# Layer 2's input sums formed a superblock ahead and kept in DRAM, and shorter durations assumed by the planner that orders the instructions

## The chip, the cores and the metric

One core of one Trainium2 chip runs the whole program. The metric is device time in microseconds (us) for one launch: 1597.66 us before, the median of 3 runs (1596.65 to 1598.69). TensorE is called PE, VectorE DVE, ScalarE ACT, GpSimd POOL and SyncE SP, as in the profile. SP does nothing but issue DMAs, in one queue, in order.

## The reference

Linear attention, then two multi-layer perceptrons, all in float32:

```python
q_s = softmax(q, axis=-1); k_s = softmax(k, axis=2)     # per head, with 1e-9 in the denominators
kv = einsum('bhsd,bhse->bhde', k_s, v)
x = einsum('bhsd,bhde->bhse', q_s, kv)                  # then heads merged: 4608 tokens x 512
h = x @ w_in1;  x = maximum(0.01 * h, h) @ w_out1       # 512 -> 2048 -> 512
h = x @ w_in2;  out = (h * sigmoid(h)) @ w_out2         # 512 -> 2048 -> 512
```

## The kernel before

The four matrix products are called layers 0 to 3. Every float32 operand is split into a rounded high part and a low part (`split2`: ACT writes the high part, line 302, DVE subtracts it to give the low part, line 298), and each product takes three matmuls (high x high, high x low, low x high). Layer 0 is done plainly (lines 665 to 667, together with the attention). Layers 1, 2 and 3 use a Strassen-like scheme with seven products, numbered 1 to 7, in place of eight. Each product needs its own operand on either side, and three or four of the seven are sums or differences of stored blocks, made by DVE (`add`, line 863).

The 4608 tokens are taken in blocks of 512, and two blocks make a superblock n. There are five, n = 0 to 4, the last with one block. In layer 2 a superblock is 4 turns i over the hidden features, and each turn has the seven products in the order 1, 2, 6, 5, 7, 4, 3. Product 1 of the next turn is pulled ahead of 4 and 3. For n = 0 to 3 each product is 12 matmuls of 512 columns: two output halves rq, two halves kq of the inner dimension, three matmuls each. For n = 4 it is 12 matmuls of 256 columns. So a superblock is 336 matmuls, and layer 2 is 1344 matmuls of 512 columns and 336 of 256 (line 1034).

The x operands of layer 2, one tile for each of 7 products and 2 halves kq, so 14 tiles, stay in SBUF for the whole superblock. The pool `r_x` has 15 such tiles (named x, xr, g, xs, xv in the profile). A tile of the next superblock can be loaded only when the last turn (i = 3) has used the tile whose place it takes.

Before the change `x_all` loads four raw blocks (1, 5, 2, 3) for each kq from the DRAM tensor `x2d`, where layer 1 has stored its output (`store1`, line 997). It loads blocks 1 and 2 a second time, as 11 and 12, into other halves of the tiles. Then DVE forms the other operands, by the table `SUMS["x"]`:

```python
"x": ((7, 3, 5, "-"), (5, 5, 11, "-"), (6, 3, 5, "-"), (4, 12, 6, "-")),
...
yield from operand(keys, "x", r, (1, 5, 3, 2, 6, 7, 4), srcs, lend, home=HOME2, used=ORDER, each=0.5)
```

So 7 = 3 - 5, then the new 5 = 5 - 11, then 6 = 3 - 5 with the new 5, then 4 = 12 - 6. The tiles are taken in the order 1, 5, 3, 2, 6, 7, 4. `split2` of an operand waits for the sums that read it, so 6 waits for the sum that makes 4.

The outputs of layer 2 go bank by bank: ACT copies a PSUM bank or DVE adds it, ACT takes Silu (`active`), and SP stores the result to `gd` (`keep`, line 1098). A bank that carries several products must be read before the next product accumulates into it (`INTO`, `AFTER`).

The order of the instructions on every engine is decided before the launch by a planner (`Queues.run`). Each task is a generator that asks for operations. The planner takes the operation that could start first on its engine, with a rank to break ties, and keeps a clock for each engine that advances by assumed durations: `v_tt`, `v_ts` (DVE), `a_` (ACT), `pe` (PE), 0.73 us to issue a DMA and 3.0 us for it to land. On the chip every queue then runs in that fixed order, and waits on semaphores.

Of the kernel before, what the change touches and what calls it, by code (L numbers as in the profile page):

```python
# [24 lines left out]


def v_tt(n):
    return 0.16 + n / 960


def v_ts(n):
    return 0.16 + n / 1920


def a_(n):
    return 0.19 + n / 1200


def g_tt(n):
# [1 line left out]


def pe(n):
    return 0.007 + n / 2330


def rank(r):
# [7 lines left out]
def wait(*keys):  # L55
    return "wait", keys
# [146 lines left out]
def linear_attention_two_mlps(  # L203
# [28 lines left out]
    P = 128  # L232
# [31 lines left out]
    merge = [2 // len(s) for s in supers]  # L264
    gd1 = [tc.dram_tile([NG, 2, 4, P, len(s), HB], F32, name=f"gda{n}") for n, s in enumerate(supers)]
    gd = [tc.dram_tile([NG, 4, len(s), P, 2, HB], F32, name=f"gd{n}") for n, s in enumerate(supers)]
    x2d = [tc.dram_tile([KD, P, 2, w], F32, name=f"x2d{n}") for n, w in enumerate(width)]

    NKV = 8
    NV = 2 * (D + 1)  # L270
# [422 lines left out]
    def act(j, f, h):  # L693
# [28 lines left out]
    }  # L722
    ORDER = (1, 2, 6, 7, 5, 3, 4)
# [3 lines left out]
    SECOND = (2, 5, 3)  # L727
    HOME = {3: (6, 1), 5: (7, 1), 2: (4, 1)}
    HOMES = HOME, {}
    HOME2 = {11: (5, 0), 12: (4, 1)}  # L730
    slot = {}

    def raw_of(key, c, home):
# [42 lines left out]
    def operand(keys, kind, r, order, srcs, give, home={}, used=(), each=0.0):  # L776

        def turn(c):
            return r + each * used.index(c) if c in used else r

        for key in keys:
            spawn(r, sums(key, kind, home, turn))
        for c in order:
            for key, src in zip(keys, srcs):
                yield rank(r)
                slot[key, c] = yield from give(c)
                done(("slot", key, c))
                for d in src:
                    if home.get(d, (d, 1))[0] == c:
                        spawn(r, fetch(key, d, home, src[d]))  # L790
                spawn(turn(c), split2(key, kind, c, home))
# [6 lines left out]
    def weight(l, i, c):  # L798
# [14 lines left out]
        src = wc[l][2 * i:2 * i + 2, :, PLANS[l][2].index(c)].rearrange("r p n -> p r n")  # L813
        yield from operand([key], "", weight_rank(l, i, c), (c,), [{c: src}], give)

    def x_all():
        for n in range(NJ):

            r, pm = at2[n, 0] - (5 if n else 4), merge[n]
            yield rank(r)  # L820
            yield wait(*(("x2", n, k, t) for k in range(0, KD, pm) for t in range(2)))
            keys, srcs = [], []
            for kq in range(2 // pm):
                keys.append(("x", 2, n, kq))
                srcs.append({})
                for c, k, t in ((1, 0, 0), (5, 0, 1), (2, 1, 0), (3, 1, 1)):
                    at = 2 * k + kq * pm
                    srcs[-1][c] = x2d[n][at:at + pm, :, t].rearrange("k p w -> p k w")
                    if c < 3:
                        srcs[-1][10 + c] = srcs[-1][c]  # L830
            yield from operand(keys, "x", r, (1, 5, 3, 2, 6, 7, 4), srcs, lend, home=HOME2, used=ORDER, each=0.5)

    def g1_all():
        for n in range(NJ):
# [110 lines left out]
                                    spawn(-100, blocks1(n, mb))  # L945

    def blocks1(n, m):
        key, pm = (1, n), merge[n]

        def product(c):  # L950
            yield wait(("p", 1, n, m, c))
            return banks[key, m, c]

        def room():
            return (yield get(r_o))

        def end(c):
            r_b.put(banks.pop((key, m, c)))

        p = yield from product(1)  # L960
        s = yield from room()
        yield op(("A", a_(TB)))
        copy("A", s, p)
        done(("kept", n, m))
        p = yield from product(6)
        yield from add(s, s, p)
        end(6)
        p = yield from product(7)
        u = yield from room()
        yield from add(u, s, p)  # L970
        end(7)
        p = yield from product(4)
        t = yield from room()
        yield from add(t, u, p)
        end(4)
        spawn(-100, store1(n, 2 + m * pm, 0, t))
        p = yield from product(2)
        t = yield from room()
        yield op(("A", a_(TB)))
        copy("A", t, p)  # L980
        banks.pop((key, m, 1))
        end(2)
        spawn(-100, store1(n, m * pm, 0, t))
        p = yield from product(5)
        yield from add(u, u, p)
        spawn(-100, store1(n, 2 + m * pm, 1, u))
        yield from add(s, s, p)
        end(5)
        p = yield from product(3)
        yield from add(s, s, p)  # L990
        end(3)
        spawn(-100, store1(n, m * pm, 1, s))

    def store1(n, k, t, o):
        pm = merge[n]
        yield op(("D", 0.73))
        nc.sync.dma_start(
            out=x2d[n][k:k + pm, :, t].rearrange("k p w -> p k w"), in_=o.rearrange("p (k w) -> p k w", k=pm)
        )
        yield wait()  # L1000
        r_o.put(o)
        done(("x2", n, k, t))

    INTO = {1: 1, 6: 1, 7: 1, 4: 1, 2: 2, 5: 5, 3: 5}
    AFTER = {6: 1, 7: 6, 4: 7, 3: 5}
# [170 lines left out]
    for j in range(NB):  # L1176
        for i in range(NG):
            at3[j, i] = t_
            t_ += 2

    def weight_rank(l, i, c):
        if l == 1:
            return at1[0, int(c in SECOND), i, 0] - 8
        return (at2[0, i] if l == 2 else at3[0, i]) - 8

    with tc.manual_schedule():
        nc.vector.memset(ones, 1.0)
        make_identity(nc, ident)
        nc.scalar.activation(out=small[0]["k"][:, 0:1], in_=ones, func=ACTF.Exp)
        for t_, t in sets:  # L1190
            t5 = t.rearrange("p (c h d) -> p c h d", c=5, h=2)
            nc.gpsimd.memset(t5[:, :, :, D:], 1.0)

            nc.gpsimd.memset(t_[SR:P, 512:640], 0.0)
            nc.gpsimd.memset(t5[SR:P, 4, :, 0:D], 0.0)
        nc.gpsimd.memset(kv_tile, 0.0)

        for n in range(NP):
            r = -40 + 5 * n
            spawn(r, k_task(n))  # L1200
            spawn(r + 1, q_task(n))
            spawn(r + 2, v_task(n))
        for n in range(NP, len(units)):
            b, j, p = units[n]
            r = -12 + 3 * p if j == 1 else step(j, 0) - 14 + 4 * p
            if b is not None:
                spawn(r, k_task(n))
                spawn(r, v_task(n))
            spawn(r, q_task(n))
        for f in range(NF):  # L1210
            spawn(-36 + 6 * f if f < 4 else step(0, f) - 4, split1(f))
            if f < NH:
                spawn(f, layer0(0, f))
        spawn(0, layer0_all())
        for t in (convert1, convert2, convert3):
            spawn(1000, t())
        spawn(0, later())
        for i, c in lead:
            spawn(weight_rank(1, i, c), weight(1, i, c))
        for l in (2, 3):  # L1220
            for i in range(NG):
                for c in ORDER:
                    spawn(weight_rank(l, i, c), weight(l, i, c))
        spawn(base[1] - 4, g1_all())
        spawn(base[2] - 5, x_all())
        spawn(base[3] - 4, g3_all())
        spawn(base[1], layers())
        qs.run()
# [30 lines left out]
```

## Time and profile before

| | |
|---|---|
| median of 3 runs | 1597.66 us |
| the profiled execution's own time | 1598.44 us |
| its span in the profile | 1596.7 us |
| PE busy | 1548.6 us (97%), 9088 matmuls |
| DVE busy | 1093.9 us (69%) |
| ACT busy | 893.5 us (56%) |
| DMA | 320.01 MB, mean 200 GB/s |

Busy time is the time in which an engine has an instruction running. Layer 0 and the attention fill the span up to 507 us, layer 1 (line 931) runs to 855 us, layer 2 (line 1034) to 1230 us, and layer 3 (line 1124) to the end. Clocks are given as a share of full speed: 1.00 is 2.4 GHz, and the lower level is 1.2 GHz.

### The profile page before, as it was taken

The page shows a single profiled execution, that of the slowest core. Times are in us where ns is not written, and L with a number is a line of the kernel's source. Part 1 is how long each engine was busy: PE and PEld are TensorE (multiplying, and loading weights), DVE is VectorE, ACT ScalarE, POOL GpSimd, SP SyncE. Part 2 cuts the span into 40 slices and gives each one's busy share as a digit, 9 for nine tenths or more (in the row PEclk, how much of TensorE's full clock was granted, in tenths as well). Part 3 has the DMA queues.
Part 4 walks back from the last instruction along what each step waited for, and adds up shares of the span by engine and source line. Part 5 has one row for each costly group of instructions (what it writes and reads, how often), then busy time and mean ns, then how long its engine had stood idle before and what let it go on. Part 6 is the DMA issues. An engine that isn't in the chain of part 4 may idle for free.

```text
span 1596.7 us, 26548 instructions
## 1 busy us (share of the span) xinstructions
PE 1548.6 (97%) x9088; PEld 1340.4 (84%) x9088; DVE 1093.9 (69%) x2046; ACT 893.5 (56%) x1965; POOL 39.4 (2%) x56
## 2 busy tenths in 40 slices
PE   5899999999999999999997999999999999999999
PEld 3687888888788888888887878787889999999998
DVE  8986756665656988888888352525267777777774
ACT  7778776685445544454556454545467444444442
POOL 2111000000000000000000000000000000000000
PEclk9999999999999999999999999999999999999999
DMA  8876778786789787878797353535369444444442
GB/s 236 267 200 179 227 228 255 227 269 194 240 268 312 234 293 217 273 219 268 230 323 269 106 185 106 185 106 175 108 195 303 133 131 133 132 133 127 134 128 70
DMA packets 281190, 320.01 MB, mean 200 GB/s; under 512 B 61408, under 2 KB 208352, under 8 KB 281056
## 3 DMA queue, kind: packets, MB, share of 16 engines
q1 hardware_dynamic: 281056, 318.32, 63.8%
q8 instruction: 72, 1.18, 0.3%
q14 instruction: 62, 0.51, 0.1%
HBM read 201.85 MB, written 116.39 MB: 199 GB/s over the span
## 4 chain that ended last, share of the span: by engine, by line
PE 90%; DVE 6%; DMA 2%; SPq 1%; issue 1%; ACT 0%; POOL 0%; DVEq 0%; POOLq 0%; ACTq 0%
PE b L1124 12%; PE h L1124 11%; PE h L1034 10%; PE b L931 10%; PE h L931 10%; PE b L1034 8%; PE h L665 8%; PE h L667 8%; PE h L666 8%; DVE o L863 2%; PE a L637 2%; DVE x L298 1%; PE a L520 1%; PE a L622 1%; DMA u<-in_k_dram 0%
## 5 line engine op out<-in xcount | busy, mean ns | idle before, releaser
L665 PE MATMUL h<-x,w 128*128 128x512 f32 x576 | 237.1, 412 | 1.9 <-ACT w L302 1.1
L666 PE MATMUL h<-x,w 128*128 128x512 f32 x576 | 224.8, 390 | 2.2 <-DVE x L298 1.6
L667 PE MATMUL h<-x,w 128*128 128x512 f32 x576 | 225.2, 391 | 0.4 <-DVE w L298 0.4
L302 ACT ACTIVATE x<-x 128x512 fp32r<-128x512 f32 x194 | 121.6, 630 | 156.8 <-DMA x<-gd 87.7
L863 DVE TENSOR_TENSOR o<-o,h 128x512 f32<-128x512 f32 x107 | 72.3, 686 | 129.1 <-ACT o L302 68.0
L698 ACT ACTIVATE o<-h 128x512 f32<-128x512 f32 x144 | 86.1, 598 | 116.4 <-PE h L667 107.4
L298 DVE TENSOR_TENSOR x<-x 128x512 fp32r<-128x512 f32 x194 | 129.6, 686 | 13.0 <-ACT x L302 10.2
L863 DVE TENSOR_TENSOR o<-o,b 128x512 f32<-128x512 f32 x118 | 79.6, 686 | 85.8 <-ACT o L302 35.4
L665 PEld LDWEIGHTS h<-x,w 128*128 128x128 f32 x576 | 108.4, 188 | 28.0 <-ACT x L645 1.8
L666 PEld LDWEIGHTS h<-x,w 128*128 128x128 f32 x576 | 108.5, 188 | 24.7 <-DVE x L298 3.2
L667 PEld LDWEIGHTS h<-x,w 128*128 128x128 f32 x576 | 108.1, 188 | 24.2 <-DVE w L298 0.8
L1034 PE MATMUL h<-x,a 128*128 128x512 f32 (+1 forms) x489 | 120.8, 379 | 6.9 <-DVE x L298 6.9
L931 PE MATMUL b<-x,a 128*128 128x512 f32 (+1 forms) x498 | 117.6, 374 | 1.2 <-DVE x L298 1.2
L931 PE MATMUL h<-x,a 128*128 128x512 f32 (+1 forms) x510 | 115.0, 364 | 0.5 <-DVE x L298 0.5
L1034 PEld LDWEIGHTS h<-x,a 128*128 128x128 f32 x489 | 88.7, 193 | 24.6 <-DVE x L298 7.7
L1124 PE MATMUL b<-a,x 128*128 128x256 f32 x816 | 107.2, 283 | 0.0
L931 PEld LDWEIGHTS b<-x,a 128*128 128x128 f32 x498 | 89.0, 188 | 18.0 <-DVE x L298 1.4
L1124 PEld LDWEIGHTS b<-a,x 128*128 128x128 f32 x816 | 102.0, 192 | 0.0
L1034 PE MATMUL b<-x,a 128*128 128x512 f32 (+1 forms) x423 | 98.4, 365 | 3.5 <-DVE x L298 3.5
L931 PEld LDWEIGHTS h<-x,a 128*128 128x128 f32 x510 | 88.1, 189 | 15.9 <-DVE x L298 0.7
L1124 PE MATMUL h<-a,x 128*128 128x256 f32 x768 | 100.8, 283 | 0.0
L302 ACT ACTIVATE x<-o 128x512 fp32r<-128x512 f32 x124 | 75.7, 625 | 42.0 <-DVE o L863 38.0
(165 smaller groups left out, 2975.9 us busy)
## 6 DMA issues: line engine op xcount, KB each, us to landing
x<-gda SPq DMA_DIRECT2D x152, 256.0 KB, 3.5
gda<-o SPq DMA_DIRECT2D x144, 256.0 KB, 2.8
gd<-o SPq DMA_DIRECT2D x144, 256.0 KB, 2.7
x<-gd SPq DMA_DIRECT2D x90, 256.0 KB, 2.7
a<-wc SPq DMA_DIRECT2D x84, 256.0 KB, 4.9
wc<-o SPq DMA_DIRECT2D x72, 256.0 KB, 3.1
raw<-in_moe_w_out_dram SPq DMA_DIRECT2D x32, 512.0 KB, 5.1
g<-gda SPq DMA_DIRECT2D x60, 256.0 KB, 3.4
```

The costliest lines, as they stand in the source:

```text
L298: engines[e].tensor_tensor(out=out_, in0=a, in1=b.bitcast(F32), op=ALU.subtract)
L302: nc.scalar.activation(out=out_, in_=in_, func=ACTF.Copy)
L520: nc.tensor.matmul(pk[o, 0:D + 1], lhsT=kc[:, o], rhs=vv[:, c, h * (D + 1):(h + 1) * (D + 1)], start=c == 0, stop=c == 4,)
L637: nc.tensor.matmul(po, lhsT=kv[bb, p], rhs=qT.rearrange("p (c t) -> p c t", c=4)[:, :, a:e], start=True, stop=True)
L665: nc.tensor.matmul(h, lhsT=w[:, 0, kk], rhs=x[:, 0], start=kk == 0, stop=False)
L666: nc.tensor.matmul(h, lhsT=w[:, 0, kk], rhs=x[:, 1], start=False, stop=False)
L667: nc.tensor.matmul(h, lhsT=w[:, 1, kk], rhs=x[:, 0], start=False, stop=kk == KD - 1)
L698: nc.scalar.activation(out=o, in_=h, func=ACTF.Prelu, alpha=0.01)
L863: nc.vector.tensor_tensor(out=o, in0=a, in1=b, op=alu)
L931: nc.tensor.matmul(banks[key, mb, c][:, mo * w_:(mo + 1) * w_], lhsT=w[:, a, at:at + P], rhs=x[:, b, z * w_:(z + 1) * w_], start=begin and ...
L1034: nc.tensor.matmul(bank[:, z * w_:(z + 1) * w_], lhsT=w4[:, a, rq * pm + z, kc], rhs=x[:, b, ko:ko + w_], start=INTO[c] == c and not (z or ...
L1124: nc.tensor.matmul(bank[:, m * HB:(m + 1) * HB], lhsT=s[:, a, at:at + P], rhs=x[:, b, r * HB:(r + 1) * HB], start=i + m + n == 0, stop=i = ...
```

## The change

Two things change. First, a new task `presums` forms the operands 7, 5, 6 and 4 of layer 2 ahead of time. For each n and kq it loads the raw blocks 3, 5, 1 and 2 from `x2d` into output tiles (`r_o`, 16 tiles shared with all other results), lets DVE make the four differences, and stores them back to `x2d`, which now has 7 blocks for each kq. It is ranked at a place one superblock ahead of their use, and for n = 0 at superblock 2 of layer 1. `x_all` then loads seven finished operands for each kq, one DMA each, in the order 1, 2, 6, 5, 7, 4, 3, and only splits them. Second, the planner's assumed durations change, which recasts the order on every engine.

```diff
 def v_tt(n):
-    return 0.16 + n / 960
+    return 0.065 + n / 960
 def v_ts(n):
-    return 0.16 + n / 1920
+    return 0.09 + n / 1920
 def a_(n):
-    return 0.19 + n / 1200
+    return 0.11 + n / 1050
 def pe(n):
-    return 0.007 + n / 2330
+    return 0.0133 + n / 2400
...
-    x2d = [tc.dram_tile([KD, P, 2, w], F32, name=f"x2d{n}") for n, w in enumerate(width)]
+    x2d = [tc.dram_tile([2 // m, 7, P, TB], F32, name=f"x2d{n}") for n, m in enumerate(merge)]
...
+    RAW2 = {(0, 0): 1, (0, 1): 5, (1, 0): 2, (1, 1): 3}
+
+    def presums():
+        for n in range(NJ):
+            for kq in range(2 // merge[n]):
+                yield rank(sum_rank(n, kq))
+                yield wait(*(("x2", n, kq, c) for c in RAW2.values()))
+                x = {}
+
+                def load(c):
+                    x[c] = yield get(r_o)
+                    yield op(("D", 0.73))
+                    nc.sync.dma_start(out=x[c], in_=x2d[n][kq, c - 1])
+
+                def keep2(c):
+                    yield op(("D", 0.73))
+                    nc.sync.dma_start(out=x2d[n][kq, c - 1], in_=x[c])
+                    yield wait()
+                    r_o.put(x.pop(c))
+                    done(("x3", n, kq, c))
+
+                yield from load(3)
+                yield from load(5)
+                yield from load(1)
+                yield wait()
+                x[7] = yield get(r_o)
+                yield from add(x[7], x[3], x[5], ALU.subtract)
+                yield from keep2(7)
+                yield from add(x[5], x[5], x[1], ALU.subtract)
+                r_o.put(x.pop(1))
+                yield from load(2)
+                yield wait()
+                yield from add(x[3], x[3], x[5], ALU.subtract)
+                yield from keep2(5)
+                x[6] = x.pop(3)
+                yield from add(x[2], x[2], x[6], ALU.subtract)
+                x[4] = x.pop(2)
+                yield from keep2(6)
+                yield from keep2(4)
+
     def x_all():
...
+            for c in (1, 2, 6, 5, 7, 4, 3):
+                for kq in kqs:
+                    yield wait(("x2" if c in (1, 2, 3) else "x3", n, kq, c))
+                    spawn(r, operand([("x", 2, n, kq)], "", r, (c,), [{c: x2d[n][kq, c - 1]}], lend))
...
+    def sum_rank(n, kq):
+        return at1[2, 0, 0, 0] + 4 * kq if not n else at2[n - 1, kq]
...
+        spawn(sum_rank(0, 0), presums())
```

Three places show how the order moves. In the rows, `x`, `xr`, `xs`, `xv` and `g` are tiles for x operands, `a` are weights, `o` are output tiles, `b` and `h` PSUM banks; the number tells one buffer from another, and x4 means four such rows in a row.

DVE at the step from superblock 0 to superblock 1 of layer 2, before. The rows on line 298 are splits (an operand read as `o` was summed), those on line 863 with `g` or `x_114` are the sums that make operand 4, and those with `b` add a bank:

```order
L298 TENSOR_TENSOR x_108<-o_156,x_108 128x512
L298 TENSOR_TENSOR xr<-xr 128x512 x2
L863 TENSOR_TENSOR o_145<-g,o_149 128x512
L863 TENSOR_TENSOR o_153<-x_114,o_148 128x512
L298 TENSOR_TENSOR x_113<-o_149,x_113 128x512
L298 TENSOR_TENSOR x_110<-o_148,x_110 128x512
L863 TENSOR_TENSOR o_143<-o_143,b 128x512
L863 TENSOR_TENSOR o_147<-o_147,b 128x512
L298 TENSOR_TENSOR g<-o_145,g 128x512
L298 TENSOR_TENSOR x_114<-o_153,x_114 128x512
```

The same place now (the line of `add` is 894):

```order
L298 TENSOR_TENSOR x_115<-x_115 128x512
L298 TENSOR_TENSOR x_108<-x_108 128x512
L894 TENSOR_TENSOR o_155<-o_155,h 128x512
L894 TENSOR_TENSOR o_149<-o_149,o_148 128x512
L298 TENSOR_TENSOR x_109<-x_109 128x512
L298 TENSOR_TENSOR x_110<-x_110 128x512
L298 TENSOR_TENSOR x_111<-x_111 128x512
L894 TENSOR_TENSOR o_154<-o_154,h 128x512
L298 TENSOR_TENSOR xr<-xr 128x512 x2
```

Before, the splits of operand 6 (`x_113`, `x_110`) stood behind the two sums that make operand 4; now the second tile of operand 2 (`x_115`), both of 6 (`x_108`, `x_109`), both of 5 (`x_110`, `x_111`) and the rest follow in PE's order, with no sum of x between them.

SP at the same step, before (loads from `x2d_101` are superblock 1's raw blocks, `gd` stores are layer 2's results):

```order
L742 DMA x_108<-x2d_101 128x512 x2
L742 DMA xr<-x2d_101 128x512 x2
L742 DMA x_109<-x2d_101 128x512
L742 DMA x_112<-x2d_101 128x512
L1098 DMA gd_95<-o_144 128x2x256
L742 DMA g<-x2d_101 128x512
L1098 DMA gd_95<-o_142 128x2x256
L742 DMA x_114<-x2d_101 128x512
L742 DMA x_115<-x2d_102 128x512
```

SP there now (line 830 stores a sum made ahead for superblock 3):

```order
L1127 DMA gd_95<-o_146 128x2x256
L740 DMA x_115<-x2d_101 128x512
L740 DMA x_108<-x2d_101 128x512
L740 DMA x_109<-x2d_101 128x512
L740 DMA x_110<-x2d_101 128x512
L740 DMA x_111<-x2d_101 128x512
L740 DMA xr<-x2d_101 128x512
L830 DMA x2d_103<-o_156 128x512
L740 DMA xr<-x2d_101 128x512
L740 DMA g<-x2d_101 128x512
```

The last raw block for operand 4 (`x_114`) used to stand behind two stores that wait for results; now a load follows a load, each for one finished operand.

SP in layer 1, superblock 2 (`gda` loads are layer 1's own operands), before:

```order
L997 DMA x2d_101<-o_155 128x512
L742 DMA x_114<-gda_92 128x512
L997 DMA x2d_101<-o_150 128x512
L742 DMA x_115<-gda_92 128x512
L742 DMA x_108<-gda_92 128x512
L742 DMA x_109<-gda_92 128x512
```

And now, a little later in the same superblock (line 826 loads raw blocks for the sums, line 830 stores a sum):

```order
L830 DMA x2d_100<-o_154 128x512
L740 DMA g<-gda_92 128x512 x3
L826 DMA o_151<-x2d_101 128x512
L740 DMA xs<-gda_92 128x512
L826 DMA o_152<-x2d_101 128x512
L740 DMA xv<-gda_92 128x512
L826 DMA o_146<-x2d_101 128x512
L740 DMA x_112<-gda_92 128x512
```

Loads and stores for the sums now lie among layer 1's own loads: up to layer 1's last operand load SP issues 20 such loads and 18 such stores, for both halves of superblocks 0 and 1 and one half of superblock 2. The other 16 loads and 18 stores lie in layer 2.

## Rows read from the trace of the kernel before

**Rows 1.** The page's 40 slices: granted PE clock, in tenths of full speed.

```profile
PEclk9999999999999999999999999999999999999999
```

**Rows 2.** Waits of PE, longest first, within 855 to 1230 us (layer 2).

```profile
PE h L1034 <- DVE x L298: 6.9, 2, 3.5
PE h L1034 <- DVE xr L298: 6.4, 1, 6.4
PE b L1034 <- DVE x L298: 3.5, 1, 3.5
PE b L1034 <- ACT o L302: 2.1, 1, 2.1
PE h L1034 <- ACT xr L302: 1.2, 1, 1.2
PE h L1034 <- DVE xv L298: 0.5, 1, 0.5
```

**Rows 3.** Windows: layers 1, 2 and 3, and the first 100 us.

```profile
507.70:855.10 347.40, 345.68 (x1682) 292.81 (x1681) 295.35 (x489) 182.68 (x310) 0.00 (x0) 1.00 0.84 265
855.10:1229.80 374.70, 354.08 (x1683) 297.24 (x1682) 185.37 (x293) 204.69 (x358) 0.00 (x0) 0.98 0.50 163
1229.80:1592.90 363.10, 363.02 (x3026) 362.82 (x3024) 260.97 (x416) 157.59 (x255) 0.00 (x0) 1.00 0.43 128
...
0.00:100.00 100.00, 78.16 (x453) 56.80 (x454) 88.62 (x209) 74.71 (x206) 17.91 (x38) 1.00 0.87 247
```

**Rows 4.** Timeline of PE, superblock 0 to 1: start, length, ... count [idle before].

```profile
913.62 4.24 PE L1034 MATMUL h<-x,a 128*128 128x512 f32 x18
917.70 0.84 PE L1034 MATMUL h<-xs,a 128*128 128x512 f32 x3
...
942.18 2.88 PE L1034 MATMUL h<-x,a 128*128 128x512 f32 x12
944.90 3.11 PE L1034 MATMUL b<-x,a 128*128 128x512 f32 x13
951.54 1.97 PE L1034 MATMUL b<-x,a 128*128 128x512 f32 x5 [3.53 <-DVE x L298]
```

**Rows 5.** Timeline of PE with 256 columns, superblock 4 of layer 2.

```profile
1196.89 1.60 PE L1034 MATMUL b<-x,a 128*128 128x256 f32 x12
1198.33 1.60 PE L1034 MATMUL h<-x,a 128*128 128x256 f32 x12
```

**Rows 6.** Timeline of PE just after the first stop of layer 2.

```profile
872.00 1.48 PE L1034 MATMUL b<-xr,a 128*128 128x512 f32 x3
873.28 1.04 PE L1034 MATMUL b<-x,a 128*128 128x512 f32 x3
```

**Rows 7.** Timeline of SP at the step from superblock 0 to 1.

```profile
944.19 1.00 SPq L742 DMA_DIRECT2D x<-x2d  x2
```

**Rows 8.** Timeline of DVE at the same step.

```profile
949.60 0.68 DVE L863 TENSOR_TENSOR o<-g,o 128x512 f32<-128x512 f32 x1
950.20 0.68 DVE L863 TENSOR_TENSOR o<-x,o 128x512 f32<-128x512 f32 x1
950.80 1.28 DVE L298 TENSOR_TENSOR x<-o,x 128x512 fp32r<-128x512 f32 x2
```

**Rows 9.** Timeline of SP at the entry to layer 2.

```profile
856.46 6.13 SPq L742 DMA_DIRECT2D a<-wc  x9
862.94 0.33 SPq L742 DMA_DIRECT2D g<-x2d  x1
```

**Rows 10.** Timeline of DVE at the entry to layer 2.

```profile
867.76 1.29 DVE L863 TENSOR_TENSOR o<-g,o 128x512 f32<-128x512 f32 x2
868.96 0.68 DVE L298 TENSOR_TENSOR xr<-o,xr 128x512 fp32r<-128x512 f32 x1
```

**Rows 11.** DMAs that load from or store to x2d, all of them.

```profile
DMA to landing us min/median/max: 2.7/4.5/6.0
```

**Rows 12.** Timeline of SP, a block of result stores in layer 2.

```profile
922.66 8.18 SPq L1098 DMA_DIRECT2D gd<-o  x8
```

More of the change, by code (lines that the diff above doesn't have):

```diff
@@ L729, in linear_attention_two_mlps @@
     HOMES = HOME, {}
-    HOME2 = {11: (5, 0), 12: (4, 1)}
     slot = {}
@@ L816, in x_all @@
     def x_all():
         for n in range(NJ):
-            r, pm = at2[n, 0] - (5 if n else 4), merge[n]
+            r = at2[n, 0] - (5 if n else 4)
             yield rank(r)
[L821 to L830, printed above, removed]
@@ L831, in x_all @@
-            yield from operand(keys, "x", r, (1, 5, 3, 2, 6, 7, 4), srcs, lend, home=HOME2, used=ORDER, each=0.5)
+            kqs = range(2 // merge[n])
+            for c in (1, 2, 6, 5, 7, 4, 3):
+                for kq in kqs:
+                    yield wait(("x2" if c in (1, 2, 3) else "x3", n, kq, c))
+                    spawn(r, operand([("x", 2, n, kq)], "", r, (c,), [{c: x2d[n][kq, c - 1]}], lend))
     def g1_all():
@@ L947, in blocks1 @@
     def blocks1(n, m):
-        key, pm = (1, n), merge[n]
+        key = 1, n
         def product(c):
@@ L975, in blocks1 @@
         end(4)
-        spawn(-100, store1(n, 2 + m * pm, 0, t))
+        spawn(-100, store1(n, m, 1, 0, t))
         p = yield from product(2)
@@ L982, in blocks1 @@
         end(2)
-        spawn(-100, store1(n, m * pm, 0, t))
+        spawn(-100, store1(n, m, 0, 0, t))
         p = yield from product(5)
         yield from add(u, u, p)
-        spawn(-100, store1(n, 2 + m * pm, 1, u))
+        spawn(-100, store1(n, m, 1, 1, u))
         yield from add(s, s, p)
@@ L991, in blocks1, with store1 @@
         end(3)
-        spawn(-100, store1(n, m * pm, 1, s))
-    def store1(n, k, t, o):
-        pm = merge[n]
+        spawn(-100, store1(n, m, 0, 1, s))
+    def store1(n, m, k, t, o):
+        c = RAW2[k, t]
         yield op(("D", 0.73))
-        nc.sync.dma_start(
-            out=x2d[n][k:k + pm, :, t].rearrange("k p w -> p k w"), in_=o.rearrange("p (k w) -> p k w", k=pm)
-        )
+        nc.sync.dma_start(out=x2d[n][m, c - 1], in_=o)
         yield wait()
         r_o.put(o)
-        done(("x2", n, k, t))
+        done(("x2", n, m, c))
     INTO = {1: 1, 6: 1, 7: 1, 4: 1, 2: 2, 5: 5, 3: 5}
```

1 row of the table SUMS is left out of this document.

## The prediction

> **What bounds the kernel now.** I read the slices first, then the waits of PE, then windows by layer, and last the timelines around the longest waits.
>
> PE is at work almost everywhere, so the time is PE's own work plus what PE loses. In the slices the granted clock looks full throughout [rows 1], but a slice is 40 us long and hides short falls, so the windows have to be read beside it. Each window gives its length, then busy time and count for PE, PEld, DVE, ACT and POOL, then the granted clock, the DMA share and GB/s. Layer 3 has PE busy for 363.02 of 363.10 us and layer 1 for 345.68 of 347.40. Layer 2 has 354.08 of 374.70, and its mean clock is 0.98 [rows 3]. The first 100 us lose 100 - 78.2 = 21.8 us to the start.
>
> Layer 2's loss is larger than its idle time. At full clock eighteen matmuls of 512 columns start over 917.70 - 913.62 = 4.08 us, 0.2267 us each [rows 4], and twelve of 256 columns over 1198.33 - 1196.89 = 1.44 us, 0.12 us each [rows 5]. Layer 2 has 1344 of the one and 336 of the other: 304.7 + 40.3 = 345.0 us. It takes 374.7, so 29.7 us are lost. Idle time is 20.6 of them, which is also the sum of the waits [rows 2]. The other 9.1 us were spent at a lower clock: just after the first stop three matmuls take 873.28 - 872.00 = 1.28 us, 0.427 us each [rows 6], which is the level of 1.2 GHz. The engine had stood still just before.
>
> The Trainium skill (Trainium Kernel Development and Optimization, section Performance Expectations) calls matmul busy time a bad metric, because matmuls are pipelined. Here the trace agrees for one more reason: a matmul at half clock counts as busy, so busy time alone would show 20.6 us to win in layer 2, and spacing shows 29.7.
>
> **Why PE stops there.** All of these waits but one (2.1 us, for ACT's copy of a bank) end with a split of an x operand [rows 2]. Take the step from superblock 0 to 1. PE ends product 3 of the old superblock at 944.90 and runs product 2 of the new one, twelve matmuls or 2.72 us. Then it starts product 6, and after one matmul stands for 3.53 us until 951.54 [rows 4]. What it lacks is the low part of operand 6, a split on DVE that starts at 950.80. Right before it DVE makes two sums for operand 4, at 949.60 and 950.20 [rows 8]. The split of 6 waits for them because 4 = 12 - 6 reads 6. They need raw block 12, whose load was issued at 944.19, as soon as product 3 let go of a tile [rows 7]. So an operand due 2.72 us after product 3 hangs on a load that can only start with product 3's end, and the path from there to the split's end (950.80 + 0.68) takes 7.3 us. Three steps have this stop, of 3.5 us each; the last step, to superblock 4, has none.
>
> At the entry to layer 2 it is worse. Raw block 12 is issued at 862.94, behind nine weight loads that hold SP from 856.46 [rows 9]. The sums follow at 867.76, the split of 6 at 868.96 [rows 10], and PE has stood for 1.2 + 6.4 us.
>
> **The change, part by part.**
>
> *The sums leave the step.* Operand 6 is loaded ready, so it waits for one load and one split. With the tiles taken in the order 1, 2, 6, 5, 7, 4, 3, which is PE's own order, and one spare tile, each second half takes the tile of the same product of the old superblock. Between a product's last use and its next use PE always runs six other products: 6 x 2.72 = 16.3 us. The path that took 7.3 us with two sums in it fits in that twice. So the three stops should go, and the entry stop with them: 20.6 - 2.1 = 18.5 us of idle time, and with it the 9.1 us at half clock, 27.6 together. The 2.1 us stay: at layer 2's end product 4 follows 7 on one bank, which the change leaves alone.
>
> *A remainder at the entry.* There DVE still has 14 splits of x, the weights' splits and the last adds of layer 1. I keep 1.0 us for it, between 0 and the 7.6 us of today. The value is near the lower end, since the 0.5 us wait for a plain split [rows 2] is the nearest row.
>
> *The sums elsewhere.* There are 36 sums before and after. Five of the nine groups of four go to layer 1: 20 x 0.60 us (the spacing of neighbouring DVE rows [rows 8]) = 12 us. DVE has 347.4 - 295.4 = 52 us free there [rows 3], and PE waits for DVE through 15 tiles. I cost it at nothing; without this cover it would be 12 us. In layer 2 DVE is busy for half of the stretch (185 of 375), and 16 sums stay there.
>
> *The extra DMAs.* Now there are 36 loads and 36 stores for the sums, and 63 operand loads in place of 54: 81 more, of 0.26 MB, 21 MB in all. In layer 1 these are 38, or 10.0 MB, beside 265 GB/s x 347.4 us = 92.1 MB. At the present rate per share (265 / 0.84 = 315 GB/s) 102.1 MB take 324 us, below the 347 that PE needs. At the rate per share of the first 100 us (247 / 0.87 = 284) they take 359.5 us, 12.1 more than now. I take 0, from the row of the stretch itself, and keep 12.1 for the range. SP issues each in 0.33 to 0.5 us [rows 7, 9], some 15 us of layer 1's 347.
>
> The Trainium skill speaks against adding such small transfers (DMA: Bandwidth & Descriptors, sections Anatomy of one DMA and Bandwidth): its fit, made on the GpSimd path, gives each DMA a fixed 2.0 us, and it asks for 1 MiB and more. By that fit one of these would take 2.6 us, an estimate from that page, and 38 of them 99 us if none overlapped. The trace shows that they do overlap, since some 350 transfers' worth of bytes pass in 347 us of layer 1.
>
> *The new order.* The shorter durations are near what the rows show: DVE advances by 0.60 us for 512 columns (now assumed 0.598, before 0.693), PE by 0.2267 and 0.12 (now 0.2266 and 0.12, before 0.2267 and 0.117). So the plan should stand closer to the chip. In layers 1 and 3 PE hardly waits today, so nothing can be won there. The start's 21.8 us may go either way, since DVE rows and PE rows change places there. I take 0, with 4 us to either side, about a fifth of what stands there.
>
> **The sum.** The profiled execution took 1598.4 us. Less 27.6, plus 1.0: 1571.8. The median of the runs lies 0.8 below that execution: **1571**.
>
> **The rivals.**
>
> *A. New stops from SP's queue.* Loads of x stand behind result stores, which wait for ACT. A block of eight took SP 8.18 us [rows 12], and a load lands in up to 6.0 us [rows 11]. With two splits' worth of work (1.3 us) that makes 15.5 us against 16.3: no stop. With a second block it would be 7.4 us late, and with some 2.3 us at half clock (9.1 over four stops) 9.7 per step. With two of three steps hit: 1571 + 19.4 = **1590**. For it: loads of the new order do stand right behind such stores. Against it: the stores there belong to the same turn whose products free the tiles. 12 in 100.
>
> *B. Slower: sums that block DVE within layer 2.* The 16 sums left there stand in DVE's queue between adds that free PSUM banks, and wait for loads that SP may issue only after a block of stores. If DVE stands for 8.2 + 6.0 = 14.2 us, the add behind it is late: PE comes back to the bank of product 5, for product 3, after seven half products, 7 x 1.36 = 9.5 us. Each of 8 load waits (two for each of four groups) would cost 4.7 + 2.3 = 7.0 us: 56 us, **1627**. It decides from 26.6 / 8 = 3.3 us a wait, or DVE standing for over 10.5 us. Against it: the load is issued before the sum is due in the plan, and a median landing is 4.5 us [rows 11]. 6 in 100.
>
> *C. DMA bounds layer 1.* At the rate of the first 100 us, worked out above: 1571 + 12 = **1583**. Against it is the stretch's own rate. 8 in 100.
>
> *D. It does not do what it says.* DVE has a burst at each step, and the splits may stand as late in the new order as the old ones did. Then the stops stay and the time is **1598**. Against it: operand 6 no longer reads the last load, and eight sums, 4.8 us, leave the burst. 6 in 100.
>
> **How the numbers follow.** The forecast has 68 in 100; its own range is 1566 (start better by 4, no remainder) to 1577. A and C add up to 1590, and with them 88 in 100 would be covered if each case were sure of its size; I end the range there, 1565 to 1590. A measurement of this kernel tells 0.2%, 3.2 us, from no change. Faster: the forecast, A and C, less 3 for a start that turns out much worse: 85. The same: 6, from D. Slower: B and what was taken off: 9.
>
> **What would show it.** Right: PE's waits on line 298 in layer 2 are gone (now line 1063), layer 2 lasts about 348 us with a clock of 1.00, DVE sums of two `o` tiles appear in layer 1, and layer 1 stays at 347 us. Wrong: stops of several us at the steps, with an x split behind a late load (A), or a wait for a bank behind a DVE sum that waits for x2d (B), or layer 1 longer with DMA share near 1 (C).

## The result, and the profile after

The changed kernel takes 1580.3 us (median of 4, 1579.17 to 1581.22) against 1598.18 (4 runs, 1596.65 to 1602.12) before: a ratio of 0.9884, with a 95% interval from 0.9865 to 0.9903. It is faster, and the time lies in the range of 1565 to 1590, but 9 us above the 1571 forecast. The profiled execution takes 1581.22 us.

The page of the changed kernel, first the head, then a group of DMA issues (count, KB each, median us from issue to landing):

```profile
span 1579.4 us, 26746 instructions
PE 1546.4 (98%) x9088; PEld 1337.7 (85%) x9088; DVE 1084.2 (69%) x2043; ACT 894.9 (57%) x1965; POOL 42.6 (3%) x59
DMA packets 291576, 341.27 MB, mean 216 GB/s; under 512 B 62704, under 2 KB 207088, under 8 KB 291440
...
x2d<-o SPq DMA_DIRECT2D x72, 256.0 KB, 3.6
```

The matmuls are the same 9088. PE's busy time fell by only 2.2 us and the span by 17.3. The DMAs move 21.3 MB more, as forecast, and `x2d` gets 72 stores, 36 of them sums. The windows tell where the time went. The rows are the first 100 us, the rest of layer 0 in two parts, then layers 1, 2 and 3; the columns are those of [rows 3]:

```profile
0.00:100.00 100.00, 75.60 (x416) 52.74 (x417) 85.67 (x202) 72.91 (x197) 18.14 (x37) 0.97 0.79 220
100.00:300.00 200.00, 197.00 (x1243) 157.43 (x1243) 131.08 (x372) 145.69 (x521) 16.96 (x16) 1.00 0.73 216
300.00:520.20 220.20, 220.20 (x1048) 179.47 (x1047) 134.62 (x284) 131.84 (x335) 7.47 (x6) 1.00 0.77 252
520.20:865.20 345.00, 345.00 (x1681) 292.57 (x1681) 306.41 (x510) 186.23 (x312) 0.00 (x0) 1.00 0.91 297
865.20:1212.60 347.40, 345.48 (x1682) 292.64 (x1681) 165.38 (x261) 200.42 (x351) 0.00 (x0) 1.00 0.62 205
1212.60:1575.40 362.80, 362.80 (x3026) 362.80 (x3024) 260.30 (x416) 157.84 (x255) 0.00 (x0) 1.00 0.43 128
```

Layer 2 lasts 347.4 us in place of 374.7 [rows 3] at a clock of 1.00: 27.3 gained. Layer 1 gains 2.2, layer 3 nothing. Layer 0 with the attention ends at 520.2, and ended at 507.9 before (cut, like all lengths below, at the first matmul of layer 1): 12.3 lost. The sum is 17.2, the difference of the two profiled executions (1598.44 - 1581.22). From 95 us to the end of layer 2, PE's list of waits (total us, times, longest) has only two rows:

```profile
PE a L488 <- DVE m L485: 2.8, 2, 2.4
PE b L1063 <- ACT o L302: 1.9, 2, 1.1
```

No wait for an x operand is left, neither at the steps nor at the entry; the second row is the bank wait that the prediction kept. At the step from superblock 0 to 1, SP, DVE and PE read (start, length, ..., count, idle before):

```profile
930.59 2.87 SPq L740 DMA_DIRECT2D x<-x2d  x5
940.07 1.30 DVE L298 TENSOR_TENSOR x<-x 128x512 fp32r<-128x512 f32 x2 [1.50 <-ACT x L302]
941.60 0.69 DVE L298 TENSOR_TENSOR x<-x 128x512 fp32r<-128x512 f32 x1 [0.23 <-ACT x L302]
944.11 4.24 PE L1063 MATMUL b<-x,a 128*128 128x512 f32 x18
948.19 2.88 PE L1063 MATMUL h<-x,a 128*128 128x512 f32 x12
```

Five operand tiles (the second of 2, both of 6 and of 5) are asked for in one run at 930.59, and the last of their splits ends at 942.29, before PE comes to any of them. Before, the split of 6 started only at 950.80 [rows 8].

The loss lies at the beginning. From 100 us on PE has work without a break in both kernels, but for 3.0 us now (200.00 - 197.00). So after 100 us it still has 507.9 - 100 = 407.9 us of work before, and 520.2 - 100 - 3.0 = 417.2 now: it is 9.3 us behind by then. Idle time is 24.4 there in place of 21.8 [rows 3], 2.6 of them; the other 6.7 is work done at the lower clock. Three stretches of 20 us, before and then after:

```profile
0.00:20.00 20.00, 7.97 (x52) 4.56 (x52) 13.33 (x35) 13.10 (x50) 6.69 (x27) 1.00 0.94 254
20.00:40.00 20.00, 15.15 (x112) 8.82 (x111) 19.27 (x46) 17.46 (x58) 3.44 (x3) 1.00 0.83 217
...
60.00:80.00 20.00, 19.60 (x86) 15.92 (x86) 18.97 (x39) 15.50 (x29) 0.00 (x0) 1.00 0.88 265
```

```profile
0.00:20.00 20.00, 5.99 (x31) 3.47 (x32) 12.03 (x33) 12.11 (x46) 5.66 (x26) 1.00 0.93 245
20.00:40.00 20.00, 16.06 (x102) 9.25 (x100) 16.45 (x41) 15.81 (x56) 4.60 (x4) 1.00 0.78 193
...
60.00:80.00 20.00, 16.68 (x81) 12.05 (x80) 19.06 (x42) 17.62 (x37) 1.32 (x1) 0.91 0.94 292
```

In the second stretch PE is busy for longer now and gets through fewer matmuls. The clock column of these rows reads 1.00 for all time ahead of the trace's first clock record, so it does not show the start. The records put TensorE at the upper level from 20.35 us on before, and only from 27.58 now; the matmuls ahead of that are spaced as at the lower level (rows below). After that the clock does not fall again in layer 0 before. Now it falls twice: at 54.88, after stops of 0.8, 1.0 and 1.2 us, and at 65.12, after one of 2.4, for 6.8 us together. Half of 7.2 + 6.8 us is 7.0, an estimate from these records that agrees with the 6.7.

One cause can be read from PE's rows. `L488` transposes the maximum of a group of keys, which DVE makes in three dependent steps (lines 479, 481, 485); `L520` is the product of exponentiated keys and values. Before:

```profile
13.33 1.14 PE L520 MATMUL a<-u,kx 128*64 128x65 f32 x16
15.67 0.45 PE L488 MATMUL a<-ident,m 128*128 128x128 f32 x1 [0.98 <-DVE k L529]
...
21.00 0.40 PE L666 MATMUL h<-x,w 128*128 128x512 f32 x1
21.23 0.40 PE L667 MATMUL h<-x,w 128*128 128x512 f32 x1
```

After:

```profile
16.19 0.45 PE L488 MATMUL a<-ident,m 128*128 128x128 f32 x1 [2.23 <-DVE m L485]
16.57 1.14 PE L520 MATMUL a<-u,kx 128*64 128x65 f32 x16
...
26.26 0.63 PE L666 MATMUL h<-x,w 128*128 128x512 f32 x1
26.68 0.78 PE L667 MATMUL h<-x,w 128*128 128x512 f32 x1
...
30.54 0.39 PE L667 MATMUL h<-x,w 128*128 128x512 f32 x1
30.77 0.40 PE L665 MATMUL h<-x,w 128*128 128x512 f32 x1
```

The planner now puts the transpose ahead of the product. PE stands 2.23 us for a maximum that is not ready, and the 20 matmuls of `L520` behind it, which before ran as soon as PE was free, come 3.24 us later. Of these, 0.55 us are no matter of order: the keys of the second group landed later in this execution (DVE's line 479 starts at 9.42, at 8.87 before). The awaited maximum is not late either: its last step on DVE ends at 16.04, at 15.53 before. It is PE's order that costs here. Matmuls of 512 columns follow each other by 0.23 us at 21.0 before; now they still take 0.42 at 26.3 and reach 0.23 only at 30.5.

### The profile page after: what moved, and what is told of

Read it like the earlier page. It is cut to its first block, busy times and chain, and to the rows that moved or that the text cites. A ratio compares the mean times of both kernels' runs of the same rounds, so it can differ in the third digit from the quotient of the medians.

```text
span 1579.4 us, 26746 instructions
## 1 busy us (share of the span) xinstructions
PE 1546.4 (98%) x9088; PEld 1337.7 (85%) x9088; DVE 1084.2 (69%) x2043; ACT 894.9 (57%) x1965; POOL 42.6 (3%) x59
## 4 chain that ended last, share of the span: by engine, by line
PE 93%; DVE 4%; DMA 2%; issue 1%; ACT 0%; SPq 0%; POOL 0%; ACTq 0%; POOLq 0%; DVEq 0%
PE h L1063 12%; PE b L1153 12%; PE h L1153 11%; PE b L962 11%; PE h L962 11%; PE b L1063 9%; PE h L667 7%; PE h L665 7%; PE h L666 7%; PE a L637 2%; PE a L520 1%; PE a L622 1%; DMA rw<-in_moe_w_in_dram 1%; DMA a<-wc 1%; DVE o L346 1%
## 5 line engine op out<-in xcount | busy, mean ns | idle before, releaser
L962 PE MATMUL b<-x,a 128*128 128x512 f32 (+1 forms) x471 | 111.9, 375 | 0.0
L1063 PE MATMUL b<-x,a 128*128 128x512 f32 (+1 forms) x498 | 108.2, 364 | 1.9 <-ACT o L302 1.9
L962 PE MATMUL h<-x,a 128*128 128x512 f32 (+1 forms) x483 | 109.2, 365 | 0.0
L1153 PE MATMUL h<-a,x 128*128 128x256 f32 x816 | 105.6, 283 | 0.0
L1153 PE MATMUL b<-a,x 128*128 128x256 f32 x792 | 101.7, 283 | 0.0
L1153 PEld LDWEIGHTS h<-a,x 128*128 128x128 f32 x816 | 101.3, 192 | 0.0
L1063 PEld LDWEIGHTS b<-x,a 128*128 128x128 f32 x498 | 85.8, 189 | 17.1 <-ACT o L302 2.3
L1063 PE MATMUL h<-x,a 128*128 128x512 f32 (+1 forms) x438 | 99.9, 372 | 0.0
L962 PEld LDWEIGHTS b<-x,a 128*128 128x128 f32 x471 | 84.6, 188 | 16.0
L1153 PEld LDWEIGHTS b<-a,x 128*128 128x128 f32 x792 | 98.0, 192 | 0.0
```

The lines of the kernel that those rows point to most:

```text
L962: nc.tensor.matmul(banks[key, mb, c][:, mo * w_:(mo + 1) * w_], lhsT=w[:, a, at:at + P], rhs=x[:, b, z * w_:(z + 1) * w_], start=begin and ...
L1063: nc.tensor.matmul(bank[:, z * w_:(z + 1) * w_], lhsT=w4[:, a, rq * pm + z, kc], rhs=x[:, b, ko:ko + w_], start=INTO[c] == c and not (z or ...
L1153: nc.tensor.matmul(bank[:, m * HB:(m + 1) * HB], lhsT=s[:, a, at:at + P], rhs=x[:, b, r * HB:(r + 1) * HB], start=i + m + n == 0, stop=i = ...
```

## Experiments

The change has two halves, so the first three runs take them apart, and test the reason for the stops by itself.

**Sums ahead, old durations.** The changed kernel with the four functions as before:

```diff
-    return 0.065 + n / 960
+    return 0.16 + n / 960
...
```

> The sums ahead alone, with the durations of before. Theory: the sums ahead take all of layer 2's stops away (layer 2 from 375 to about 347 us) and the new durations cost 12 us at the start and in layer 0, by another order there. This kernel has before's own order of PE through all of layer 0, so layer 0 should end at about 508 us and the time be 1598 - 27 - 2 = about 1569 us. Rival 1: the removal of the stops needs the better durations too; then layer 2 keeps several us of stops and the time is 1575 to 1590. Rival 2: the 12 us of layer 0 come from the sums' DMAs or tiles and not from the durations; then layer 0 still ends at 520 us and the time stays at 1580.

Measured: 1576.02 us (1574.47 to 1577.85), ratio 0.9857 [0.9842, 0.9871]. Its median is some 4 us below that of the whole change, with intervals that just overlap. Layer 0 ends at 509.4, layer 2 lasts 347.9. But layer 1 lasts 350.5, with these waits of PE and two of 0.3 us, where before PE waited for 1.7 us in all:

```profile
PE h L962 <- DVE x L298: 2.5, 2, 1.4
PE h L962 <- DVE g L298: 1.0, 2, 0.8
```

So the sums alone remove layer 2's stops, and with the old durations they cost 3.3 us in layer 1. The theory's 1569 was missed by 7 us, most of it there.

**New durations, sums as before.** The kernel before with the four functions of the change.

> The new durations alone, with the sums of layer 2 made at the step as before. Theory: layer 0 ends at about 520 us, as in the changed kernel, since PE's order there is the same; layer 2 keeps its stops; the time is 1598 + 12 - 2 = about 1608 us, slower than before. Rival 1: better durations remove part of the stops in layer 2, then 1590 to 1600. Rival 2: layer 0 ends at 508 us and the time is about 1597.

Measured: 1604.37 us (8 runs, 1601.27 to 1607.39), ratio 1.0031 [1.0021, 1.0042]: slower than before by 0.3%. Layer 0 ends at 520.5, layer 1 lasts 344.9, layer 2 373.3 with its stops in place:

```profile
PE h L1034 <- DVE x L298: 8.9, 2, 4.6
PE h L1034 <- DVE g L298: 3.8, 1, 3.8
PE b L1034 <- DVE x L298: 3.6, 1, 3.6
```

The 12 us of layer 0 belong to the durations, whatever is done with the sums: 520.5 here against 507.9 before, and 520.2 against 509.4 with the sums ahead.

**The stop's chain, cut at one place.** In the kernel before, operand 6 is split without waiting for the sum of 4; its tile is given back later, once that sum has read it:

```diff
-                if any(d == c or home.get(d, (d, 1))[0] == c for d in u[1:3])
+                if any(d == c or home.get(d, (d, 1))[0] == c for d in u[1:3]) and not (kind == "x" and c == 6)
...
+        done(("op", key, c))
+        if kind == "x" and c == 6:
+            yield wait(("sum", key, 3))
...
-        done(("op", key, c))
```

> Before's kernel with one wait taken out: the split of operand 6 in layer 2 no longer waits for the sum that makes operand 4; the tile that holds 6 is given back after that sum. The sums stay at the step, in the same number. Theory (the stop is the chain from the late raw block through the sum of 4 to the split of 6): the 3.5 us stops and the long stop at the entry go or shrink to under 1 us each, layer 2 takes 347 to 355 us, the time is about 1575. Rival (the stop is the burst of work on DVE at the step): stops of 2 to 3.5 us stay, layer 2 takes over 365 us, and the time is 1590 or more.

Measured: 1578.19 us (1577.85 to 1578.36), ratio 0.9870 [0.9854, 0.9887]. The three stops at the steps are gone with all sums still in place; layer 2 lasts 353.3, and of the 5.1 us of idle time that remain 4.3 stand at its entry. The two longest are still over the 1 us that the theory allowed:

```profile
PE h L1036 <- ACT x L302: 1.6, 1, 1.6
PE h L1036 <- ACT xr L302: 1.5, 1, 1.5
```

This shows that the stops at the steps came from the wait of 6 for the sum of 4, not from the amount of DVE work there; at the entry some of the wait has another cause. A few lines bring 21.4 of the 27.3 us, with no byte of extra traffic.

**Each half where it helps.** The changed kernel, planned with the old durations until the last product of layer 0 is placed, then with the new:

```diff
+EARLY = [True]
...
-    return 0.065 + n / 960
+    return (0.16 if EARLY[0] else 0.065) + n / 960
...
+        if f == NF - 1 and j == NB - 1:
+            EARLY[0] = False
```

> The changed kernel, but the planner uses before's durations until it has placed the last product of layer 0, and the new ones from there on. Theory: layer 0 as before (it ends at about 508 us), layers 1 to 3 as in the changed kernel (345, 347 and 363 us), so about 1569 us, faster than both kernels and than the sums alone (1576). Rival: the gain of the new durations in layer 1 (350 to 345 us) hangs on the order that layer 0 leaves behind (where weight conversion stands); then layer 1 stays at about 350 us and the time at 1575.

Measured: 1570.84 us (1570.15 to 1573.59), ratio 0.9838 [0.9823, 0.9852]. Layer 0 ends at 509.9, layers 1 and 2 last 346.1 and 349.0. Its interval lies wholly below that of the change. It lands on the prediction's 1571, which had no loss in layer 0.

**Is it the assumed landing time?** The changed kernel with 4.5 us to land in place of 3.0:

```diff
-DMA_LATENCY = 3.0
+DMA_LATENCY = 4.5
```

> The changed kernel with 4.5 us assumed for a DMA to land, in place of 3.0. Theory 1: the new durations harm layer 0 because shorter work leaves the too short DMA latency uncovered, so that DVE is sent to data that has not landed; with 4.5 us layer 0 ends at 512 us or earlier and the time is about 1572. Theory 2: any recast of the dense start costs some 5 to 12 us against an order that was good by selection; then layer 0 ends at 515 to 522 us here too, and the time is 1575 to 1583.

Measured: 1577.91 us (1577.18 to 1580.65), ratio 0.9884 [0.9868, 0.9901]. Layer 0 ends at 517.7: at most 2.5 of the 12.3 us came back, and the first 100 us have PE busy for 73.2 us only. Too short a landing time is not what loses the start.

**Longer durations still.** DVE's and ACT's durations raised above the old ones (0.255 + n / 960, 0.23 + n / 1920, 0.27 + n / 1200), PE's as before:

> The changed kernel with durations longer than before's for DVE and ACT, by 0.095 and 0.08 us. Theory 1 (short durations harm the start): layer 0 ends at 508 us or earlier, as good as before. Theory 2 (any recast costs): layer 0 ends at 513 us or later. In both, layer 1 gets stops, since DVE seems full to the planner: over 350 us.

Measured, one execution: 1615.22 us. Layer 0 ends at 511.9, between the two theories, so this run does not decide between them. But layer 1 lasts 383.5, with these waits among others:

```profile
PE h L962 <- DVE x L298: 9.9, 4, 4.5
PE h L962 <- DVE xs L298: 5.8, 1, 5.8
PE b L962 <- DVE x L298: 5.7, 2, 3.9
```

With the changed kernel and the one with the old durations this is a series in the assumed time of a DVE operation of 512 columns (the other durations change along with it): at 0.598 us layer 1 lasts 345.0, at 0.693 it lasts 350.5, at 0.788 383.5. If all of layer 1's DVE instructions counted as 512 columns, the plan would see 510 x 0.598 = 305 us of DVE work, 501 x 0.693 = 347 and 515 x 0.788 = 406, where PE needs 345; before, without the sums, 489 x 0.693 = 339. That the plan takes DVE for the bound as soon as its sum passes PE's is worked out from this and was not read from the plan itself. In the chip's records DVE is busy for only 302 to 307 us in all three.

**Which duration.** Four kernels set one group to the new value and leave the others old. Both of DVE's:

> The changed kernel with only DVE's durations new; ACT's and PE's are before's. Theory 1 (DVE's durations carry it): layer 0 ends at 516 us or later, layer 1 takes 345 us. Theory 2 (any recast costs): layer 0 also ends late, so this run alone does not tell; the next two, with ACT's and PE's alone, do. If ACT's durations carry it, layer 0 ends at 510 us or earlier here.

Measured, one execution: 1577.75; layer 0 ends at 516.3, layer 1 lasts 346.2. Only ACT's:

> The changed kernel with only ACT's durations new. With DVE's alone layer 0 ended at 516.3 us. If DVE's carry the loss, it ends at 510 to 513 us here; if any recast costs as much, at 515 us or later. Layer 1: if DVE's durations removed its stops, it keeps about 350 us here.

Measured, one execution: 1576.04; layer 0 ends at 510.1, layer 1 lasts 351.3. PE's order differs from before's from 20.4 us on here (line 622 ahead of 520), so a recast order does not by itself cost 5 to 12 us, as the second theory of the landing-time run had it. Only PE's:

> The changed kernel with only PE's durations new, which leaves PE's first 253 rows as before. Layer 0 ends at 509 to 511 us by either theory, since the first 100 us are before's; layer 1 keeps about 350 us if DVE's durations are what removes its stops.

Measured, one execution: 1574.75; 509.2 and 350.5. And only `v_tt`, the DVE duration for two tensors, without that of the weights' decoding steps (`v_ts`):

> The changed kernel with only one of DVE's two durations new, that of instructions with two tensors (additions and splits); that of the weight decoding's single-tensor ones, ACT's and PE's are before's. With both of DVE's new, layer 0 ended at 516.3 us and layer 1 took 346.2. Theory (the decoding, placed too early, is what DVE stands for): layer 0 ends at 511 us or earlier here, and layer 1 still takes about 346 us. Rival (the two-tensor instructions carry both): layer 0 ends at 515 us or later, layer 1 takes 346.

Measured, one execution: 1577.05; layer 0 ends at 517.2 and layer 1 lasts 344.9, layer 2 346.4:

```profile
0.00:100.00 100.00, 76.29 (x423) 53.42 (x424) 85.46 (x205) 73.77 (x200) 17.67 (x37) 0.97 0.79 226
...
517.20:862.10 344.90, 344.90 (x1681) 292.60 (x1680) 306.21 (x511) 187.37 (x312) 0.00 (x0) 1.00 0.90 296
```

So one number does both: `v_tt` repairs layer 1 and carries 9.3 of the 12.3 us that layer 0 loses. The loss does not need the new `v_ts`. The decoding of the weights is not cleared by this run, though, since two of its four steps on DVE (lines 346 and 352) are planned with `v_tt`. Kernels with before's order of PE all through layer 0 end it between 507.9 and 509.9, and before itself is the lowest of them, so one or two us of such a figure are scatter.

**Where in layer 0.** The old durations are kept for the first 95 us of the plan only:

> The changed kernel with before's durations until the plan has placed six features of block 1 in layer 0, which keeps before's order of PE for its first 251 rows, the first 95 us or so; the new ones from there. Theory: of layer 0's 12.3 us, about 9.5 (idle time and half clock) lie in the first 100 us and 3 near 250 us; layer 0 ends at 510 to 513 us. Rival: the order after 100 us carries it; layer 0 ends at 516 us or later.

Measured, one execution: 1574.37; layer 0 ends at 511.9, and its second stretch shows

```profile
100.00:300.00 200.00, 197.25 (x1247) 159.01 (x1246) 132.99 (x373) 150.73 (x546) 16.90 (x15) 1.00 0.73 217
```

The 2.75 us lost behind 100 us appear as in the changed kernel (3.0 there), while the rest stays away: most of the loss, 8.3 of 12.3, is made in the first 95 us.

**Both at once.** The kernel with old durations in layer 0, and 4.5 us to land from layer 1 on:

```diff
-                task[2], task[5] = begin, begin + cost + DMA_LATENCY
+                task[2], task[5] = begin, begin + cost + (DMA_LATENCY if EARLY[0] else 4.5)
```

> Before's durations until the last product of layer 0 is placed, then the new ones and 4.5 us assumed for a DMA to land. The kernel with 4.5 us throughout had layer 1 at 345.0 and layer 2 at 345.9 us, the one with 3.0 us 346.1 and 349.0. If the longer latency carries that, layers 1 and 2 take 345 and 346 us here, layer 0 ends at 509 us, and the time is about 1567; if those 4 us were chance, the time stays at 1571.

Measured: 1569.14 us (1568.77 to 1569.84), ratio 0.9819 [0.9803, 0.9835], the lowest of all, though its interval overlaps that of the kernel with old durations in layer 0 alone. Layers 1 and 2 last 344.9 and 346.0, as the first reading had it, while the time lies between the two; from 95 us to the end PE's list of waits has one row:

```profile
PE b L1068 <- ACT o L305: 0.7, 1, 0.7
```

## Why the prediction was right or wrong

*What bounds, and why PE stops.* Right, and shown by the run that frees operand 6: the stops hung on the chain product 3, load of 12, two sums, split of 6. The half clock went with the idle time: layer 2 gained 27.3 us, 18.7 of it idle (20.62 - 1.92), the rest clock. The forecast was 27.6 less 1.0.

*The remainder at the entry.* Taken as 1.0, measured as none for x. Layer 2 lasts 347.4 where 345.0 + 2.1 + 1.0 = 348.1 were forecast.

*The sums elsewhere, at nothing.* Right as the change stands (layer 1 lasts 345.0), but not for the reason given. DVE's free 52 us were there with the old durations too, and layer 1 still lost 3.3: an engine with free time on the chip can be full in the plan that sets its order. I had not asked what the plan would make of the added work.

*The extra DMAs, at nothing.* Right. Layer 1 moves 297 GB/s x 345.0 us = 102.5 MB at a share of 0.91, and PE has no wait there. The rule of the Trainium skill that spoke against small transfers (DMA: Bandwidth & Descriptors, section Bandwidth) does not decide here, since the 256 KB transfers overlap.

*The new order.* This is the step that failed: "I take 0, with 4 us to either side". It measured -2.2 in layer 1 and +12.3 in layer 0, 10.1 together, which is the distance from the forecast of 1571.8 to the profiled 1581.2 but for the 0.7 that layer 2 did better. That 1580 still lies within 1565 to 1590 is luck: the forecast's own range ended at 1577, and the rest was kept for rivals A and C, which did not come about. The 21.8 us to which the 4 were a fifth are idle time alone. That the start also runs at the lower clock, until 20.35 us before, was not in them, because the clock column read 1.00.

The argument was that the shorter durations are near the rows, "so the plan should stand closer to the chip". They are near the spacing of independent DVE instructions. The rows of the changed kernel's DVE at the later stop in layer 0, and PE's stop itself:

```profile
248.73 0.43 DVE L337 TENSOR_SCALAR o<-o 128x512 f32<-128x512 f32 x1 [5.41 <-ACT o L335]
...
252.33 0.41 DVE L479 TENSOR_TENSOR o<-u 128x256 f32<-128x256 f32 x1
252.78 0.29 DVE L481 TENSOR_TENSOR m<-o 128x128 f32<-128x128 f32 x1
253.10 0.28 DVE L485 TENSOR_TENSOR m<-m,u 64x128 f32<-64x128 f32 x1
253.31 0.41 DVE L479 TENSOR_TENSOR o<-u 128x256 f32<-128x256 f32 x1
```

```profile
253.53 0.30 PE L488 MATMUL a<-ident,m 128*128 128x128 f32 x1 [2.42 <-DVE m L485]
```

From 479 to 481 and from 481 to 485, each of which reads the one before, it is 0.45 and 0.32 us. From 485 to the next group's 479, which does not, it is 0.21. The new `v_tt` gives 0.332 for 256 columns and 0.198 for 128, right for the second kind; the old one gives 0.427 and 0.293, close to the first kind. In layers 1 to 3 DVE works through independent splits and sums, and the short figure is the true one. The attention at the start is chains from DVE to PE and back. There the three steps take 0.45 + 0.32 + 0.28 = 1.05 us, and the plan now counts 0.73 for them (1.01 before), so it expects the maximum 0.3 us too early. PE is set to wait for it, with work that is ready behind, as the rows at 16.19 and 16.57 show. That the 0.3 us turned this order was not read from the plan. At 253 they are the small part: the chain is queued behind a weight's decoding, for which DVE stood 5.41 us.

How much of the 9.3 us comes from this stays open. The run with both DVE durations new has the old order at 13 us and still loses 8.4 in layer 0, so there are other places. Its clock reaches the upper level only at 30.22 us, the latest of all runs, after stops of 0.9, 0.8 and 0.7 us from 15 to 20.5. The planner does have a second figure: 0.1 us between a result and its reader (`LATENCY`, line 69). But line 120 takes it off when the reader is on the same engine, which is where the rows show 0.11 us more. A planner that keeps it there, with the short spacing, was not tried.

*The rivals.* None of A to D came about: no stop behind a store (A), none behind a sum in layer 2 (B), layer 1 not longer (C), and the stops did not stay (D). The loss was of a kind that the list did not hold. A slower case built on the recast start would have been the useful one, and the run with new durations alone shows that it has a mechanism: +0.3% by itself.

## What to carry to other kernels

When a planner sets the order, an assumed duration is two numbers: how soon the engine is free, and how soon the result can be read. Here the figure that is true for a stream of independent work was too short for a chain, and the one close to a chain came with stops in a layer where DVE was not full. How far these two misfits carry the loss and the stops is argued here, not shown. Read the clock of a start from the spacing of the matmuls too, not from the clock column alone. Ask of every work added to a covered engine whether the plan, too, has room for it, and where a stop hangs on a single wait, try to cut that wait before moving work and bytes elsewhere.

## What the runs showed of the hardware

DVE instructions in the start are sometimes much longer than others of their form. In both kernels 16 single rows of the first 320 us exceed the median of their form by over 0.25 us, and every one of them begins while POOL works on two tensors (lines 591, 615) and ends 0.15 to 0.6 us behind it. From the changed kernel, DVE and then POOL:

```profile
11.92 1.15 DVE L341 TENSOR_SCALAR o<-o 128x512 uint32<-128x512 uint32 x1
...
30.07 0.27 DVE L502 TENSOR_TENSOR u<-u,a 64x128 f32<-64x128 f32 x1
...
34.81 1.02 DVE L481 TENSOR_TENSOR m<-o 128x128 f32<-128x128 f32 x1
```

```profile
11.56 1.23 POOL L615 TENSOR_TENSOR o<-o,rq 128x512 f32<-128x512 f32 x1 [5.84 <-DVE k L492]
...
29.74 1.04 POOL L615 TENSOR_TENSOR o<-o,rq 128x512 f32<-128x512 f32 x1 [8.28 <-DMA uq<-in_q_dram]
...
34.45 1.23 POOL L615 TENSOR_TENSOR o<-o,rq 128x512 f32<-128x512 f32 x1
```

Line 481 takes 0.29 us elsewhere and 1.02 here, ending at 35.83, 0.15 after POOL. Line 341 takes 0.43 elsewhere and 1.15 here, ending 0.28 after POOL's end at 12.79. It goes the other way round too: line 337 at 20.13, beside a POOL instruction that starts at 20.12, keeps its 0.43, and POOL takes 1.33 in place of the 1.04 above. Line 502, which reads one operand from a PSUM bank (`a`), keeps its 0.27 at 30.07 within POOL's instruction. The Trainium skill (SBUF — State Buffer, section Who interferes with whom) says just this: DVE and GpSimd share one pair of ports as an exclusive lock, taken by a DVE instruction with two SBUF inputs or in a two-port mode. The trace agrees: 481 and 341 wait for POOL's end, and 502, with one SBUF input, does not. That 341 and 337 run in such a mode no run here shows; they read one tensor and take 0.43 us for 512 columns, where a two-tensor instruction takes 0.68. The excess adds up to 11.3 us of DVE time before and 9.5 now, so its sum is no cause of the difference; but it lies in the start, where DVE's chains hold PE up, and no plan with fixed durations sees it. Moving this work off POOL was not tried.

The second surprise is the price of standing still at the start. There 2.6 us more of idle time came with 6.7 us lost to the lower clock, where layer 2 before the change had 20.6 with 9.1. At the start a stop of 2.23 us, ended at 16.19, came ahead of a rise to the upper level that is 7.2 us later; that this stop alone put it off is not shown.
